# Attention with part of its exponentials made on VectorE, in a statically scheduled rewrite

## The chip, the cores and the metric

One core of one Trainium2 chip. The metric is device time in microseconds (us) from start to end of one execution; lower is better. Engines carry the profile's short names where lines of it are shown: PE (TensorE, matrix multiply), PEld (its weight loads), ACT (ScalarE), DVE (VectorE), POOL (GpSimd), SP (the queue that starts transfers). A ratio below is the mean time of one kernel's fast runs over that of the other's fast runs of the same rounds, so it is not quite the ratio of the medians that are quoted.

## The reference, cut to what matters

Two attention branches over the same input, 2048 positions, 512 features, 32 heads of 16, mixed by a gate.

```python
q, k, v = ...(x @ A_wqkv)                       # branch A: full attention
scores = einsum("bhqd,bhkd->bhqk", q, k) * (16 ** -0.5)
a = einsum("bhqk,bhkd->bhqd", softmax(scores), v) ... @ A_wo
# branch B: the same with 8 keys per query (every second of the last 16 positions)
b = ... @ B_wo
g = sigmoid((x * gate_w).sum(-1))
return g * a + (1 - g) * b
```

Branch A needs 32 x 2048 x 2048 exponentials. The kernels count them in units of 128 keys x 512 queries of one head; there are 2048 units. Branch B is small and runs on GpSimd beside it.

## The kernel before

A unit is a score matmul (32 rows of the array, one of four row positions), an exponential, and a value matmul (17 of 32 columns, one of four column positions) that adds into an accumulator. Three units share one exponential instruction. All of branch A's exponentials run on ScalarE.

```python
def emit_qk(k, dup):                            # one set of three units
    ring = ps.tile([128, maxn, QW], FP32, tag=("rA" if k % 2 == 0 else "rB"), ...)
    for s_, (c_, i, t, j) in enumerate(us):
        mm(ring[:, s_, :], kt_all[32*j:32*j+32, i, t*128:(t+1)*128], qt[32*j:32*j+32, :], True, True, ...)
    pT = work.tile([128, maxn, QW], BF16, tag="pT", ...)
    A.activation(out=pT[:, 0:nu, :], in_=ring[:, 0:nu, :], func=ACT.Exp, scale=float(DH) ** -0.5)

def emit_junk():                                # "filler": nobody reads the result
    jt = misc_ps([128, QW])
    mm_ct(jt, ident[:], ones_t[:], True, True)  # four matmuls, one per column position

# in the loop over sets, where no projection work is at hand:
    if cost < cfg["fill_min"] and k < nsets:
        emit_junk()
```

The order of every engine's instructions is fixed at build time by a loop over the sets. PSUM holds two score buffers of three banks, one scratch bank and the accumulator.

Of the kernel before, what the change touches and what calls it, by code (L numbers as in the profile page):

```python
# [1 line left out]

# [10 lines left out]
BF16 = mybir.dt.bfloat16  # L13
PSUM = bass.MemoryType.PSUM

CFG = dict(
    set_units=3,
    pt_bufs=4,
    burst_budget=2,
    fill_min=1,  # L20
    pv_lag=2,
    enable_b=True,
    chain=("pe", "dve", "act", "pool", "sp"),
    split_dma=False,
)

H = 32
DH = 16
# [4 lines left out]
NEG = -1.0e9  # L33


def _ap(base, dims):
    return bass.AP(tensor=base.tensor, offset=base.offset, ap=[list(d) for d in dims])


@with_exitstack  # L40
def kernel(
# [12 lines left out]
    cfg = CFG  # L54
# [3 lines left out]
    assert D == 512 and S % QW == 0  # L58
# [4 lines left out]
    NBG = S // 32  # L63
    BPC = QW // 32
    ENB = cfg["enable_b"]
    SU = cfg["set_units"]
# [5 lines left out]
    def misc_ps(shape, dtype=FP32, tag="misc"):  # L72
        return ps.tile(shape, dtype, tag=tag, bufs=1, name="misc_ps")
# [4 lines left out]
    def chain_on(key, bi):  # L78
        if bi is None or not hasattr(bi, "ins"):
            return bi  # L80
        if key in cfg["chain"] and prev_inst.get(key) is not None:
            tc.add_manual_dep(bi.ins, prev_inst[key].ins.name, dep_info, reason="program order")
        prev_inst[key] = bi
        return bi

    def chain(bi):
        return chain_on("pe", bi)
# [12 lines left out]

    V = Chained(nc.vector, "dve")
# [4 lines left out]
    def mm(out, lhsT, rhs, start, stop, **kw):  # L106
        return chain(nc.tensor.matmul(out, lhsT=lhsT, rhs=rhs, start=start, stop=stop, **kw))  # L107

    def mm_ct(out, lhsT, rhs, start, stop):
        for c4 in range(4):  # L110
            mm(out[32 * c4:32 * c4 + 32], lhsT[:, 32 * c4:32 * c4 + 32], rhs, start, stop, tile_position=(0, 32 * c4))
# [4 lines left out]

    wst = const.tile([128, DC, 3 * D], BF16, name="wst")
    a_w3 = A_wqkv.rearrange("(c p) n -> p c n", p=128)
    xld_tiles = {}

    def load_x_chunk(sc):
        if sc < 2:
            xl = work.tile([128, W, D], BF16, name="xld", tag="ksh", bufs=2)
        else:
            xl = work.tile([128, NG, QW], BF16, name="xld2", tag="oat", bufs=2)
        eng = SP if (sc % 2 == 0 or not cfg.get("split_dma", True)) else G
        eng.dma_start(out=xl[:, 0:TPC, :], in_=x2d[sc * QW:(sc + 1) * QW, :].rearrange("(t p) d -> p t d", p=128))
        xld_tiles[sc] = xl

    SP.dma_start(out=wst[:, :, D:2 * D], in_=a_w3[:, :, D:2 * D])  # L130
    for sc in range(min(NC, 4)):
        load_x_chunk(sc)
    SP.dma_start(out=wst[:, :, 0:D], in_=a_w3[:, :, 0:D])

    def late_loads():
        SP.dma_start(out=wst[:, :, 2 * D:3 * D], in_=a_w3[:, :, 2 * D:3 * D])
        with nc.allow_non_contiguous_dma(reason="tiny gate vector load"):
            SP.dma_start(out=gw[:], in_=gate_w.rearrange("(c p) -> p c", p=128))
        if ENB:
            SP.dma_start(out=bw[:], in_=B_wqkv.rearrange("(c p) n -> p c n", p=128))  # L140
            SP.dma_start(out=bwo[:], in_=B_wo.rearrange("(c p) n -> p c n", p=128))
        for i in range(NG):
            for j in range(4):
                r0 = (4 * i + j) * DH
                SP.dma_start(out=woarr[32 * j:32 * j + DH, i, :], in_=A_wo[r0:r0 + DH, :])
        if ENB:
            SP.dma_start(out=kv_scr[0:16, 0:D], in_=woarr[16:32, 0, :])
            SP.dma_start(out=kv_scr[0:16, D:2 * D], in_=woarr[16:32, 1, :])

    gw = const.tile([128, DC], BF16, name="gw")  # L150
    if ENB:
        bw = const.tile([128, DC, 3 * D], BF16, name="bw")
        bwo = const.tile([128, DC, D], BF16, name="bwo")
        kv_scr = tc.dram_tile([16 + S, 2 * D], BF16, name="kv_scr")
    woarr = const.tile([128, NG, D], BF16, name="woarr")
    G.memset(woarr[:], 0.0)

    ident = const.tile([128, 128], BF16, name="ident")
    make_identity(nc, ident[:])
    identf = const.tile([NT, NT], FP32, name="identf")  # L160
    make_identity(nc, identf[:])
    ones_t = const.tile([128, QW], BF16, name="ones_t")
    V.memset(ones_t[:], 1.0)
    z32 = const.tile([128, 32], BF16, name="z32")
    V.memset(z32[:], 0.0)
# [5 lines left out]
    for j in range(4):  # L171
        V.memset(selq[32 * j:32 * j + DH, 32 * j + DH:32 * j + DH + 1], 1.0)

    xT = const.tile([128, DC, S], BF16, name="xT")
    kt_all = const.tile([128, NG, S], BF16, name="kt_all")
    vp_all = const.tile([128, NT, H, DH + 1], BF16, name="vp_all")
    G.memset(vp_all[:, :, :, DH:DH + 1], 1.0)
# [3 lines left out]
    g_sp = const.tile([128, NT], FP32, name="g_sp")  # L181
    if ENB:
        omg = const.tile([128, NT], FP32, name="omg")
        maskb = const.tile([128, H, W], FP32, name="maskb")
        G.memset(maskb[:], 0.0)
        G.affine_select(out=maskb[:], in_=maskb[:], compare_op=ALU.is_ge, fill=NEG,
                                base=0, pattern=[[0, H], [-DIL, W]], channel_multiplier=1)

    def k_proj_job(i, sc, ps_tag="misc"):
        st = {}  # L190

        def part(c0, c1, last):
            def s():
                if c0 == 0:
                    st["pk"] = misc_ps([128, QW], tag=ps_tag)
                    mm_init(st["pk"], e32, QW)
                pk = st["pk"]
                for c in range(c0, c1):
                    for j in range(4):
                        h = 4 * i + j  # L200
                        mm(pk[32 * j:32 * j + DH, :], wst[:, c, D + h * DH:D + (h + 1) * DH],
                           xT[:, c, sc * QW:(sc + 1) * QW], False, c == DC - 1, tile_position=(0, 32 * j))
                if last:
                    V.tensor_copy(out=kt_all[:, i, sc * QW:(sc + 1) * QW], in_=pk[:])
                    V.tensor_reduce(out=kmax_all[:, i, sc:sc + 1], in_=kt_all[:, i, sc * QW:(sc + 1) * QW],
                                    axis=AX.X, op=ALU.max, apply_absolute_value=True)
            return s
        return [(3, part(0, 2, False), 0, True), (2, part(2, DC, True), 0, False)]

    def selk_job(i):  # L210
        def s():
            V.tensor_reduce(out=kmax[:, i:i + 1], in_=kmax_all[:, i, :], axis=AX.X, op=ALU.max)
            V.tensor_scalar(out=selk_all[:, i, :], in0=selq[:], scalar1=kmax[:, i:i + 1], scalar2=-1.0,
                                    op0=ALU.mult, op1=ALU.mult)
        return [(0, s, 0, False)]

    def v_proj_job(h0, h1, tb, TB, ps_tag="misc"):
        nh = h1 - h0
        n = nh * DH
        assert TB * n <= 512  # L220
        cost = max(1, (TB * DC * max(n, 96)) // 512)
        st = {}

        def mk(half):
            def s():
                if half == 0:
                    st["pv"] = misc_ps([128, TB, n], tag=ps_tag)
                pv = st["pv"]
                for tt in range(half * TB // 2, (half + 1) * TB // 2):
                    t = tb + tt  # L230
                    for c in range(DC):
                        mm(pv[:, tt, :], xT[:, c, t * 128:(t + 1) * 128],
                           wst[:, c, 2 * D + h0 * DH:2 * D + h1 * DH], c == 0, c == DC - 1)
                if half == 1:
                    V.tensor_copy(out=vp_all[:, tb:tb + TB, h0:h1, 0:DH],
                                  in_=pv[:].rearrange("p t (h d) -> p t h d", d=DH))
            return s
        if TB == 1:
            def s1():
                mk(0)()  # L240
                mk(1)()
            return [(cost, s1, 0, False)]
        return [(max(1, cost // 2), mk(0), 0, True), (max(1, cost - cost // 2), mk(1), 0, False)]

    qt_tiles = {}

    def q_proj_job(c_, i, ps_tag="misc"):
        st = {}

        def s1():  # L250
            p1 = misc_ps([128, QW], tag=ps_tag)
            st["p1"] = p1
            mm_init(p1, z32, QW)
            for c in range(2):
                for j in range(4):
                    h = 4 * i + j
                    mm(p1[32 * j:32 * j + DH, :], wst[:, c, h * DH:(h + 1) * DH],
                       xT[:, c, c_ * QW:(c_ + 1) * QW], False, False, tile_position=(0, 32 * j))

        def s2():  # L260
            p1 = st["p1"]
            for c in range(2, DC):
                for j in range(4):
                    h = 4 * i + j
                    mm(p1[32 * j:32 * j + DH, :], wst[:, c, h * DH:(h + 1) * DH],
                       xT[:, c, c_ * QW:(c_ + 1) * QW], False, c == DC - 1, tile_position=(0, 32 * j))
# [688 lines left out]
```

## Time and profile before

Median 1026.06 us of three runs (1018.97 to 1027.02).

| before | value | where it is read |
|---|---|---|
| ScalarE busy | 937.0 of 1019.7 us | engine table |
| one exponential set of three | 1491 ns long; 1.36 us from start to start | groups; 929 us / 683 |
| ScalarE busy from 200 to 800 us | 96% | stretches |
| filler matmuls | 1156 (289 groups of four) | groups |
| granted clock | 0.973 | cores |

One group of VectorE that has two inputs in SBUF, in a 200 us stretch with GpSimd 88% busy and in one with GpSimd idle (grouped lines of the kernel before for 200 to 400 us, then for 800 to 1000 us):

```profile
L98 DVE SCALAR_TENSOR_TENSOR absq<-qt 128x512 bf16<-128x512 bf16 x7 | 8.1, 1161 | 0.2
```

```profile
L98 DVE SCALAR_TENSOR_TENSOR absq<-qt 128x512 bf16<-128x512 bf16 x6 | 4.2, 692 | 0.2
```

The same operation takes 1161 ns beside a busy GpSimd and 692 ns beside an idle one.

### The profile page before, as it was taken

The page shows a single profiled execution, that of the slowest core. Times are in us where ns is not written, and L with a number is a line of the kernel's source. Part 1 is how long each engine was busy: PE and PEld are TensorE (multiplying, and loading weights), DVE is VectorE, ACT ScalarE, POOL GpSimd, SP SyncE. Part 2 cuts the span into 40 slices and gives each one's busy share as a digit, 9 for nine tenths or more (in the row PEclk, how much of TensorE's full clock was granted, in tenths as well). Part 3 has the DMA queues.
Part 4 walks back from the last instruction along what each step waited for, and adds up shares of the span by engine and source line. Part 5 has one row for each costly group of instructions (what it writes and reads, how often), then busy time and mean ns, then how long its engine had stood idle before and what let it go on. Part 6 is the DMA issues. An engine that isn't in the chain of part 4 may idle for free.

```text
span 1019.7 us, 20777 instructions
## 1 busy us (share of the span) xinstructions
PE 761.0 (75%) x8981; PEld 237.9 (23%) x8981; DVE 331.3 (32%) x535; ACT 937.0 (92%) x703; POOL 597.4 (59%) x540
## 2 busy tenths in 40 slices
PE   5887888877787867777777777776777877777775
PEld 2333232322222211121222221111122211111122
DVE  3453655454244423133233423212222311101113
ACT  1787999999999999999899999999999999999995
POOL 2006699878988979989978878997960000000000
PEclk9999999999999999999899999979999999999998
DMA  7002114003103213102200140310100000000000
GB/s 238 23 2 84 63 43 146 2 22 126 51 7 100 74 52 125 42 2 83 94 2 22 63 135 1 125 42 2 42 1 7 17 1 1 1 1 1 2 1 21
DMA packets 44388, 47.52 MB, mean 47 GB/s; under 512 B 2260, under 2 KB 41732, under 8 KB 44296
## 3 DMA queue, kind: packets, MB, share of 16 engines
q1 hardware_dynamic: 44296, 46.19, 13.9%
q8 instruction: 70, 1.15, 0.5%
q14 instruction: 22, 0.18, 0.1%
HBM read 39.86 MB, written 6.33 MB: 45 GB/s over the span
## 4 chain that ended last, share of the span: by engine, by line
ACT 49%; issue 24%; PE 19%; DVE 8%; ACTq 0%; DMA 0%; POOL 0%; POOLq 0%; DVEq 0%
ACT pT L98 48%; PE misc_ps L107 8%; PE ring L107 5%; PE acc L107 5%; DVE accT L98 2%; DVE kt_all L98 1%; DVE ott L98 1%; DVE qt L98 1%; ACT ex L98 1%; PE pxt L594 0%; DVE oat L98 0%; ACT xT L98 0%; PE misc_ps L462 0%; DVE osb L98 0%; DVE lg L98 0%
## 5 line engine op out<-in xcount | busy, mean ns | idle before, releaser
L98 ACT ACTIVATE pT<-ring 128x1536 bf16<-128x1536 f32 (+1 forms) x683 | 929.0, 1490 | 52.9 <-PE ring L107 50.8
L107 PE MATMUL ring<-qt,kt_all 32*128 32x512 bf16 x2048 | 266.1, 390 | 114.6 <-ACT pT L98 113.6
L107 PE MATMUL acc<-pT,vp_all 128*17 128x512 bf16 x2048 | 288.3, 392 | 79.8 <-ACT pT L98 79.4
L98 POOL TENSOR_TENSOR prod<-prod 128x512 f32<-128x512 f32 x192 | 227.2, 1197 | 5.0
L98 POOL TENSOR_TENSOR prod<-ksh,qb 128x512 f32<-128x512 bf16 x128 | 148.0, 1187 | 94.5 <-DVE qb L98 78.3
L107 PE MATMUL misc_ps<-ones_t,ident 128*32 128x512 bf16 x1156 | 171.6, 399 | 3.9 <-DVE obt L98 3.5
L98 POOL TENSOR_TENSOR prod<-vsh,attn 128x512 f32<-128x512 bf16 x128 | 140.8, 1131 | 53.6 <-issue 38.4
L107 PEld LDWEIGHTS <-kt_all 32*128 32x128 bf16 x2048 | 69.4, 91 | 340.1 <-issue 338.8
L107 PEld LDWEIGHTS <-vp_all 128*17 128x17 bf16 x2048 | 78.6, 89 | 269.8 <-issue 256.2
L98 DVE STREAM_TRANSPOSE accT<-acc 128x512 f32<-128x512 f32 x32 | 22.8, 714 | 209.6 <-PE acc L107 209.6
L107 PE MATMUL misc_ps<-xT,wst 128*16 128x512 bf16 x1024 | 81.6, 385 | 5.3 <-ACT xT L98 3.2
L107 PE MATMUL misc_ps<-bw,xT 128*32 128x512 bf16 x768 | 61.3, 386 | 3.9 <-DVE kvs L98 1.8
L98 DVE CAST qt<-misc_ps 128x512 bf16<-128x512 f32 x32 | 22.1, 690 | 113.1 <-PE misc_ps L107 113.1
L107 PE MATMUL misc_ps<-woarr,oat 128*32 128x512 bf16 x512 | 42.3, 401 | 2.6 <-DVE oat L98 2.6
L98 POOL TENSOR_TENSOR ob<-prod 128x512 f32<-128x512 f32 x32 | 41.7, 1304 | 2.5
L107 PEld LDWEIGHTS <-xT 128*32 128x32 bf16 (+1 forms) x1088 | 34.7, 97 | 29.1 <-issue 21.5
L98 DVE CAST kvs<-misc_ps 128x512 bf16<-128x512 f32 x32 | 22.1, 689 | 52.1 <-PE misc_ps L107 52.1
L107 PEld LDWEIGHTS <-ident 128*32 128x32 bf16 x1156 | 33.8, 95 | 15.1 <-issue 13.7
L107 PEld LDWEIGHTS <-wst 128*16 128x16 bf16 x1024 | 29.5, 89 | 32.0 <-issue 14.7
L98 DVE CAST kt_all<-misc_ps 128x512 bf16<-128x512 f32 x32 | 22.1, 690 | 38.3 <-PE misc_ps L107 38.3
L98 DVE TENSOR_TENSOR ott<-accT,rden 128x512 bf16<-128x512 f32 x32 | 32.3, 1009 | 1.1
L98 DVE TENSOR_TENSOR qt<-qt,misc_ps 128x512 bf16<-128x512 bf16 x32 | 22.0, 687 | 30.3 <-PE misc_ps L107 30.3
(71 smaller groups left out, 420.9 us busy)
## 6 DMA issues: line engine op xcount, KB each, us to landing
ksh<-kv_scr SPq DMA_DIRECT2D x16, 1024.0 KB, 7.3
vsh<-kv_scr SPq DMA_DIRECT2D x16, 1024.0 KB, 6.5
kv_scr<-kvs SPq DMA_DIRECT2D x16, 256.0 KB, 2.0
out_dram<-osb SPq DMA_DIRECT2D x16, 128.0 KB, 1.7
wst<-in_A_wqkv_dram SPq DMA_DIRECT2D x3, 512.0 KB
bw<-in_B_wqkv_dram SPq DMA_DIRECT2D x1, 1536.0 KB
xld<-in_A_x_dram SPq DMA_DIRECT2D x2, 512.0 KB, 5.4
xld_70<-in_A_x_dram SPq DMA_DIRECT2D x1, 512.0 KB, 6.7
```

Of the source, the lines that this page charges most:

```text
L98: return chain_on(key, f(*a, **k))
L107: return chain(nc.tensor.matmul(out, lhsT=lhsT, rhs=rhs, start=start, stop=stop, **kw))
```

## The change

The intent is to take ScalarE's load down. For some key tiles, all four heads of a group (four units, called a quad here) are made on VectorE instead. Scaling the score and adding a constant, then storing it as a 16-bit integer, gives the bit pattern of a bf16 number that approximates the exponential: exponent right, mantissa linear. Four such patterns, shifted by different constants, are multiplied by the same values on PE, which adds them up; the sum is smoother than one pattern. I worked its ripple out from the constants: 0.4% at most about its mean.

The order is no longer made by a loop over sets but by a list scheduler that runs at build time with durations of its own, an event simulation inside the kernel file. The filler is gone, except that the rewrite adds 13 groups of four matmuls at the very start (tile `warm`, 52 matmuls). The diff is 2029 lines; this is its core.

```diff
-CFG = dict(set_units=3, pt_bufs=4, burst_budget=2, fill_min=1, pv_lag=2, ...)
+OFFS = (0, 21, 52, 91)
+EXP_MULT = 128.0 * math.log2(math.e) * DH ** -0.5
+EXP_ADD = 128.0 * (127.0 - _mean_log_ratio())
+SHARED = 1.35                      # planned stretch of an addition beside GpSimd
...
+    def make_quad(p, t):
+        for j in range(4):
+            def fill(...):          # score of one head into a scratch bank
+                mm(st["s"][:], kt_all[32*j:32*j+32, i, t*128:(t+1)*128], qt_tiles[...][32*j:32*j+32, :], ...)
+            def conv(...):          # the first bit pattern
+                V.tensor_scalar(out=q["terms"][0][:, j, :], in0=st["s"][:], scalar1=EXP_MULT, scalar2=EXP_ADD,
+                                op0=ALU.mult, op1=ALU.add)
...
+        for k in range(1, len(OFFS)):
+            def term(k=k):          # the shifted ones
+                V.tensor_scalar(out=q["terms"][k][:], in0=q["terms"][0][:], scalar1=float(OFFS[k]), scalar2=None, op0=ALU.add)
+            tops.append(S_.add(Op("DVE", term, dur=610.0 * SHARED + 80.0, ...)))
...
+        for k, term in enumerate(q["terms"]):
+            for j in range(4):
+                emit_pv_mm(p, t, j, term[:, j, :].bitcast(BF16), ...)
...
-    def emit_junk():
-        jt = misc_ps([128, QW])
-        mm_ct(jt, ident[:], ones_t[:], True, True)
...
+        res = "rA" if ring_i[0] == 0 else "rB"     # score buffers of 3 and 2 banks, two scratch banks
+        n = 3 if ring_i[0] == 0 else 2
...
-        V.tensor_tensor(out=ott[:], in0=accT[:], in1=rd_bc, op=ALU.mult)
+            (V if last else G).tensor_tensor(out=ott[:], in0=st["accT"][:], in1=rd_bc, op=ALU.mult)
...
+        while b_next[0] < NT and b_next[0] * 1.9 <= p + 0.5:    # pace of branch B
+            b_tile(b_next[0], now + 2000.0)
```

## The prediction

> **What bounds it now.** ScalarE. In the page's engine table it is busy 937.0 of 1019.7 us (92%). 683 exponentials of three 128x512 units hold it 929 us, so one set of three costs 1.36 us when back to back (each lasts 1.49 us in the groups, but they overlap). The stretches table shows the loss outside: about 31 us before the first set, then 144 of 160 us busy up to 200 us, 97% from 200 to 1000 us, and 12 us of tail. PE is 75% busy, but 1156 of its 8981 matmuls are filler and transposes. VectorE is 32% busy, GpSimd 59% and idle after 760 us. PE would become the limit only if the change adds passes.

> **What the change does.**
> - It moves whole key tiles ("quads", four units) from ScalarE to VectorE. ScalarE drops about 0.46 us per unit (sets of 3 and 2: 1.36 and about 0.94 us, from the measured slope), so 1.85 us per quad.
> - VectorE per quad: four PSUM conversions of 128x512 (0.69 us each as for the other evictions, about 0.61 when they overlap) = 2.5 us, and three 16-bit additions of a constant over 128x2048.[...]
> - PE per quad: four lone score fills and sixteen value matmuls in place of four, about 1.3 us more by pass length (estimate). The filler goes.
> - VectorE's other work falls from 331 to roughly 260 us: the scaling of the output moves to GpSimd, the second final eviction and one bound pass go.
> - The score buffers shrink from 3+3 to 3+2 banks, for a second scratch bank.

> **How many quads.** Balancing ScalarE, (2048-4N)x0.46+~45 us of ends, with VectorE, 260+4.9N, gives N about 100 and 785-800 us if nothing contends and the order fits.

> **What contends.** [...] absq takes 1161 ns between 200 and 400 us, where GpSimd is 88% busy, and 692 ns after 800 us, where it is idle. So each addition should last about 1.0-1.2 us while GpSimd works, against the 0.9 us the new schedule assumes, adding 0.3-1 us per quad[...]. The instruction order is fixed at build time, so late additions stall PE, and PE then starves ScalarE. PE itself is nearly full. I charge 50-60 us for this.

> **Prediction.** 850 us, 8 in 10 between 790 and 925. Faster by over 2%: 0.93; within 2%: 0.04; slower: 0.03.

> **What would show it.** Groups: about 80-115 quads, i.e. 320-460 conversions of about 0.69 us and 240-345 additions with mean 0.9-1.2 us in GpSimd's stretch and about 0.7 outside it; exponential sets of two and three, about 1600-1700 units. Engine table: ScalarE 87-95% busy, VectorE 80-95%, GpSimd 75-90% with its work spread to nearly the end. Chain of waits: ScalarE falls below its 49%; VectorE and PE grow. First exponential set at 20-30 us.

> **What would make it wrong.** [...] If contention is mild and the schedule fits, 790-810 us. If PE's changes between row and column tiling cost more than planned, ScalarE idles waiting for scores.

The sum came to 785-800 us for the balance, taken as 795, plus a charge of 50-60 us, taken as 55: 850 us. Of the 4.9 us a quad in the balance, 2.5 are the conversions; the other 2.4, by difference, are for the three additions, and no run had shown one. That additions lengthen beside GpSimd as absq does was my assumption. The other unit costs can be read in the trace of the kernel before: VectorE operations of 0.69 us follow each other in 0.60 to 0.61 us where the later one does not wait for the earlier, and PE passes of 512 columns, four matmuls side by side, follow each other in 0.216 us at full clock (by estimate four lone fills and four passes of values in place of two passes, so six more, 1.3 us).

## More of the kernel before

"Granted clock" is the share of full speed that the profile's clock records give for PE.

From the page of the kernel before, the engine table and the time line in 40 equal slices (each digit is the busy share in tenths; PEclk is the granted clock in tenths):

```profile
PE 761.0 (75%) x8981; PEld 237.9 (23%) x8981; DVE 331.3 (32%) x535; ACT 937.0 (92%) x703; POOL 597.4 (59%) x540
...
PE   5887888877787867777777777776777877777775
...
DVE  3453655454244423133233423212222311101113
ACT  1787999999999999999899999999999999999995
POOL 2006699878988979989978878997960000000000
PEclk9999999999999999999899999979999999999998
```

ACT reads 9 nearly everywhere: ScalarE is the limit. DVE is two thirds idle, which is the room that the change wants to use. POOL is dense for three quarters of the time.

The costliest group and the filler, from the page of the kernel before (columns: line, engine, operation, tiles, shapes, count | busy us, mean ns | idle before, and what ended it):

```profile
L98 ACT ACTIVATE pT<-ring 128x1536 bf16<-128x1536 f32 (+1 forms) x683 | 929.0, 1490 | 52.9 <-PE ring L107 50.8
...
L107 PE MATMUL misc_ps<-ones_t,ident 128*32 128x512 bf16 x1156 | 171.6, 399 | 3.9 <-DVE obt L98 3.5
```

## The result, and the profile after

The change runs in 976.36 us (median of 4, 971.36 to 978.63) against 1023.99 us for the kernel before in the same rounds: ratio 0.9529 (95% interval 0.9485 to 0.9574), faster. Executions over 1.5% slower than the fastest of the same kernel are left out of the means. The prediction of 850 us was too low by 126 us, and the result lies outside its range of 790 to 925 us.

From the page of the changed kernel, the same lines as above:

```profile
PE 826.1 (85%) x8922; PEld 250.4 (26%) x8922; DVE 772.8 (79%) x1097; ACT 796.8 (82%) x709; POOL 690.5 (71%) x570
...
PE   7989878998899889888899888889889988987961
...
DVE  3757699898887998789897788889787869799760
ACT  3868748999888889998999878897989978898850
POOL 1340679849589796367984689769686499699686
PEclk9989988999689987887989786796879979798695
```

No row is 9 throughout any more. ScalarE has 140 us less to do, but its idle time did not fall with it: its busy share went from 92 to 82%. PEclk has fallen from 9 to between 5 and 9; the mean is 0.863 against 0.973. The chain of waits of this page can't be used: it stops after 2% of the span.

The groups that answer to those of before, and the two new groups of VectorE (page of the changed kernel):

```profile
L300 ACT ACTIVATE pT<-ring 128x1024 bf16<-128x1024 f32 (+2 forms) x683 | 784.8, 1264 | 127.7 <-PE ring L300 107.0
...
L300 DVE TENSOR_SCALAR dt<-dt 128x2048 uint16<-128x2048 uint16 x261 | 305.9, 1208 | 2.3
L300 DVE TENSOR_SCALAR dt<-m_ps 128x512 uint16<-128x512 f32 x348 | 231.4, 682 | 90.3 <-PE m_ps L300 59.6
```

348 conversions and 261 additions are 87 quads. ScalarE's idle time before exponentials went from 53 to 128 us, and 107 us of it ended when PE delivered scores. An addition took 1208 ns.

What a half-speed stretch looks like (time line of the changed kernel, first PE, then ScalarE; start us, length us of the group, engine, what, [idle before, and what ended it]):

```profile
607.05 0.60 PE L300 MATMUL m_ps<-qt,kt_all 32*128 32x512 bf16 x1
607.06 1.03 PE L300 MATMUL ring<-qt,kt_all 32*128 32x512 bf16 x3
608.01 0.62 PE L300 MATMUL m_ps<-ones_t,zpad 128*32 128x512 bf16 x4
608.41 1.07 PE L300 MATMUL m_ps<-xT,wq 128*16 128x512 bf16 x8
609.42 0.61 PE L300 MATMUL ring<-qt,kt_all 32*128 32x512 bf16 x2
...
613.67 0.40 PE L300 MATMUL acc<-pT,vp_all 128*17 128x512 bf16 x4
614.00 0.39 PE L300 MATMUL m_ps<-qt,kt_all 32*128 32x512 bf16 x2
```

```profile
606.69 1.02 ACT L300 ACTIVATE pT<-ring 128x1024 bf16<-128x1024 f32 x1 [2.06 <-PE ring L300]
608.18 1.45 ACT L300 ACTIVATE pT<-ring 128x1536 bf16<-128x1536 f32 x1 [0.47 <-PE ring L300]
610.12 1.02 ACT L300 ACTIVATE pT<-ring 128x1024 bf16<-128x1024 f32 x1 [0.49 <-PE ring L300]
```

What additions and GpSimd products look like beside each other (time line of the changed kernel, first VectorE, then GpSimd):

```profile
703.19 3.01 DVE L300 TENSOR_SCALAR dt<-dt 128x2048 uint16<-128x2048 uint16 x2
```

```profile
703.06 5.62 POOL L300 TENSOR_TENSOR prod<-vsh,lg 128x512 f32<-128x512 bf16 x4
```

Two additions take 3.01 us and four GpSimd products take 5.62 us, 1.40 each. An addition takes 0.70 us with GpSimd emptied (e2, below), a product 1.07 us in a stretch of the kernel before where VectorE is mostly idle (4.27 us for four).

The end of the changed kernel (time line of ScalarE, GpSimd and PE): the last exponential of branch A ends at 941 us, and then

```profile
930.98 10.06 ACT L300 ACTIVATE pT<-ring 128x1536 bf16<-128x1536 f32 x9 [1.15 <-PE ring L300]
...
957.06 4.26 POOL L300 TENSOR_TENSOR prod<-vsh,lg 128x512 f32<-128x512 bf16 x4
961.28 3.82 POOL L300 TENSOR_TENSOR prod<-prod 128x512 f32<-128x512 f32 x3
965.17 1.26 POOL L300 TENSOR_TENSOR obb<-ob,prod 128x512 bf16<-128x512 f32 x1
...
966.49 0.62 PE L300 MATMUL m_ps<-ident,obb 128*32 128x128 bf16 x16 [19.05 <-POOL obb L300]
```

PE waits 19 us for GpSimd to end the last tile of branch B. The tail after the last exponential is 34 us; in the kernel before it was 10 us. The tail differs much between the runs below, so the end of the last exponential and the tail have to be read apart.

The scheduler gives a yardstick of its own. Its event simulation, which runs when the kernel is built, ends at 879 us for the changed kernel, with 87 quads, VectorE busy 672 us and PE 615 us. It assumes full clock and an addition of 0.90 us. So the chip ran 97 us later than the plan. Below, "plan" means this number; it is arithmetic of the kernel file, not a measurement, and it is trusted here only because runs below land near it (e1 2% over, e5 1% under, e10 2% over).

### The profile page after: what moved, and what is told of

It is laid out like the page before. It is cut to its first block, busy times and chain, and to the rows that moved or that the text cites. A ratio compares the mean times of both kernels' runs of the same rounds, so it can differ in the third digit from the quotient of the medians.

```text
span 975.1 us, 21187 instructions
## 1 busy us (share of the span) xinstructions
PE 826.1 (85%) x8922; PEld 250.4 (26%) x8922; DVE 772.8 (79%) x1097; ACT 796.8 (82%) x709; POOL 690.5 (71%) x570
## 5 line engine op out<-in xcount | busy, mean ns | idle before, releaser
L300 ACT ACTIVATE pT<-ring 128x1024 bf16<-128x1024 f32 (+2 forms) x683 | 784.8, 1264 | 127.7 <-PE ring L300 107.0
L300 PE MATMUL ring<-qt,kt_all 32*128 32x512 bf16 x1700 | 319.7, 424 | 69.5 <-ACT pT L300 65.4
L300 DVE TENSOR_SCALAR dt<-dt 128x2048 uint16<-128x2048 uint16 x261 | 305.9, 1208 | 2.3
L300 DVE TENSOR_SCALAR dt<-m_ps 128x512 uint16<-128x512 f32 x348 | 231.4, 682 | 90.3 <-PE m_ps L300 59.6
L300 POOL TENSOR_TENSOR prod<-prod 128x512 f32<-128x512 f32 (+1 forms) x208 | 268.2, 1301 | 5.8
L300 POOL TENSOR_TENSOR prod<-vsh,lg 128x512 f32<-128x512 bf16 x128 | 161.5, 1291 | 96.5 <-issue 94.9
L300 PE MATMUL acc<-pT,vp_all 128*17 128x512 bf16 x1700 | 182.0, 424 | 0.0
L300 PE MATMUL m_ps<-qt,kt_all 32*128 32x512 bf16 x348 | 132.5, 439 | 15.6 <-DVE dt L300 12.2
L300 PE MATMUL acc<-dt,vp_all 128*17 128x512 bf16 x1392 | 118.6, 466 | 5.1 <-DVE dt L300 5.0
L300 PE MATMUL m_ps<-bw,xT 128*32 128x512 bf16 x768 | 58.2, 404 | 2.2 <-DVE kvs L300 1.8
```

What stands on the lines that cost most here:

```text
L300: return chain_on(key, f(*a, **k))
```

## The experiments

Theories. **Contention** (the expectations call it the port theory; no run shows by what means it comes about): additions and GpSimd's operations make each other longer (1.21 us for an addition on the mean, 1.40 us for a product, as above), VectorE and branch B run late against the fixed order, and the in-order engines wait. **Clock**: without the filler, PE has stretches of little work, its clock is halved there, and then PE is too slow to feed ScalarE. **Order**: the rewritten order is bad in itself. All edits are to the changed kernel unless said otherwise, and each was timed in 3 rounds. Medians of before in the same rounds were 1022 to 1027 us.

| run | edit | us | ratio to before | clock | plan |
|---|---|---|---|---|---|
| the change | | 976.36 | 0.9529 | 0.863 | 879 |
| e1_no_quads | no quads | 1476.98 | 1.4407 | 0.651 | 1446 |
| e2_no_gpsimd | branch B emptied on GpSimd (wrong result) | 914.85 | 0.8914 | 0.879 | 879 |
| e3_zero_filler | filler | 959.38 | 0.9359 | 0.950 | 892 |
| e4_before_no_filler | kernel before, filler off | 1055.77 | 1.0297 | 0.788 | |
| e5_no_gpsimd_filler | e2 and e3 (wrong result) | 883.85 | 0.8641 | 0.994 | 892 |
| e6_scale_on_vector | output scaling back on VectorE | 985.05 | 0.9605 | 0.848 | 865 |
| e7_honest_additions | additions planned at 1.21 us | 1006.98 | 0.9837 | 0.832 | 923 |
| e8_selective_filler | filler only where the plan is thin | 966.78 | 0.9453 | 0.869 | 881 |
| e9_wide_values | value matmuls 32 columns wide | 977.98 | 0.9536 | 0.854 | 879 |
| e10_two_terms_filler | two patterns per quad, filler | 867.91 | 0.8483 | 0.976 | 853 |
| e11_decoupled | nobody waits for branch B (wrong result) | 961.37 | 0.9360 | 0.855 | 879 |
| e12_two_terms | two patterns per quad | 928.06 | 0.9113 | 0.863 | 866 |
| e13_filler_same_order | filler unknown to the scheduler | 973.43 | 0.9514 | 0.949 | 879 |
| e14_no_gpsimd_filler_same_order | e2 and e13 (wrong result) | 906.03 | 0.8831 | 0.967 | 879 |

### The rewrite without quads

```diff
-        if e == "PE" and d_busy[0] < 2:
+        if False and e == "PE" and d_busy[0] < 2:
```

> The rewrite with no unit moved to VectorE (all 2048 exponentials on ScalarE, sets of 3 and 2). If the rewritten order is sound in itself, ScalarE bounds it: 410 pairs of sets x 2.30 us + about 45 us of ends = 985 to 1010 us, ScalarE over 93% busy. If the rewritten order itself (lost filler, 3+2 banks) starves ScalarE, over 1030 us with the granted clock clearly under the 0.973 of before. Clock theory: PE has less to do here than in the change and no filler, so the clock is at or under 0.86. Port theory: [...] VectorE is never late and the clock should be near 0.97.

It took 1477 us at a clock of 0.651. By number that is the second expectation (over 1030 us, a low clock), but by a cause that I had not named. The plan itself is 1446 us: without quads the scheduler makes an order in which ScalarE waits 350 us for the small softmax of branch B, and PE 368 us for GpSimd. So this run says nothing about clock or contention. It says that the order is not robust: the list scheduler turned a lighter problem into a plan 567 us longer, and the chip followed the plan to about 2%.

### Emptying GpSimd

The order of all other engines is unchanged; 33 GpSimd operations per tile of branch B become two memsets.

```diff
+            fn = lg_zero if n_ == 17 else obb_zero if n_ == 32 else (lambda: None)
             o = Op("POOL", fn, dur=dur, ...)
```

> Wrong result on purpose: the changed kernel in its exact order, but GpSimd's 33 operations per tile of branch B are replaced by two memsets, [...] branch B is never late. Port theory: additions fall from 1208 to about 690 ns, VectorE is never late, the clock returns to over 0.95 and the time to 830 to 870 us. Clock theory (the lost filler alone lowers the clock): additions fall likewise, but the clock stays under 0.90 and the time is 900 to 950 us (only the 20 us of GpSimd tail and some VectorE time come back).

914.85 us, 61 us less, with the clock at 0.879. The group of additions (grouped lines of this run):

```profile
L300 DVE TENSOR_SCALAR dt<-dt 128x2048 uint16<-128x2048 uint16 x261 | 173.2, 701 | 2.3
```

701 ns against 1208 ns: the additions are longer because GpSimd works, as the contention theory has it, and GpSimd's work is worth 61 us in all (the waits for branch B included). Its further claim, that the low clock is only a consequence, fell: the clock hardly moved. The clock theory had named this outcome. 36 us are left over the plan.

### The filler put back

Four matmuls with zero weights add nothing to the accumulator ahead of each batch of value matmuls; the scheduler knows of them.

```diff
+        for j in range(4):
+            mm(acc_tiles[periods[p]][32*j:32*j+32, :], z32, ones_t[:], False, False, tile_position=(0, 32*j))
         for (_, t, j, _, grp, s_) in batch:
```

> The changed kernel with a filler put back: four matmuls by zero weights accumulate nothing into the value accumulator ahead of each batch of value matmuls (about 425 groups, 92 us more PE work at full clock, known to the scheduler). Clock theory: granted clock back over 0.95, time 900 to 945 us in spite of the extra work. Port theory: the clock may rise, but PE only gets more work and the time stays at 970 to 1010 us.

The 92 us are an estimate: 425 passes of 0.216 us, the planned length of a pass, which is also what the traces of before and the change show at full clock.

The clock came back to 0.950 and the time fell to 959.38 us, between the ranges of the two theories (900 to 945 and 970 to 1010 us). The filler is PE work too (about 425 groups). The trace says where the gain lies: the last exponential still ends at 939 us (941 in the change; with 85 quads ScalarE has 8 units, about 4 us, more to do), and the tail is 18 us instead of 34. From 200 to 800 us (the change, then this run; columns: us, then busy us and instruction counts of PE, PEld, DVE, ACT, POOL, then clock, DMA share, GB/s):

```profile
200.00:800.00 600.00, 529.24 (x5524) 150.32 (x5527) 505.20 (x698) 531.38 (x471) 442.15 (x357) 0.85 0.15 46
```

```profile
200.00:800.00 600.00, 542.00 (x6637) 155.77 (x6640) 494.11 (x682) 533.42 (x472) 459.18 (x375) 0.95 0.16 48
```

ScalarE ran 471 and 472 instructions in these 600 us. So beside a working GpSimd the higher clock gave ScalarE next to nothing; this run's gain is an earlier end of branch B, under another plan.

### The kernel before without its filler

```diff
     def emit_junk():
+        return
```

> The kernel before without its 289 minus 0 filler groups (matmuls whose result nobody reads). Clock theory: the granted clock falls from 0.97 to under 0.90 and the time rises by 1 to 6%. Rival: filler only fills idle PE time, clock over 0.95, time within 1% of 1024 us or lower.

1055.77 us, 3.0% slower, with the clock at 0.788. Nothing else in the source differs, and the tail is 10 us in both, so this is the cleanest evidence for the clock theory: less PE work made this kernel slower. In the change the filler went too, with no line of my sum for it. The stretch from 200 to 800 us of the kernel before, then of this run (columns: us, then busy us and instruction counts of PE, PEld, DVE, ACT, POOL, then clock, DMA share, GB/s):

```profile
200.00:800.00 600.00, 450.09 (x5310) 130.56 (x5307) 192.04 (x309) 576.65 (x437) 491.03 (x439) 0.97 0.16 52
```

```profile
200.00:800.00 600.00, 472.31 (x4351) 123.03 (x4345) 191.88 (x305) 561.37 (x422) 492.42 (x442) 0.76 0.16 51
```

959 matmuls fewer, and yet PE is busy longer and ScalarE less.

### Both losses removed

> Wrong result on purpose: GpSimd's branch B emptied as in e2 and the zero filler of e3. The scheduler's own plan for this order ends at 892 us. If the plan plus these two losses (port, clock) account for the change's time, it lands on its plan: 890 to 905 us, clock over 0.95, ScalarE waiting under 60 us for scores. If a third loss of the size of the other two is left, 925 us or more.

883.85 us at a clock of 0.994, 8 us under its plan of 892 us and 6 us below the expected range. No third loss shows between plan and chip. It is not excluded, though: the plan counts 0.90 us for an addition and a working branch B, and this run had 0.71 us and none. The filler is worth 31 us here against e2 (884 and 915 us), and here it is ScalarE that gains: the last exponential ends at 867 us against 897. From 200 to 800 us e2 had

```profile
200.00:800.00 600.00, 540.17 (x5822) 155.08 (x5813) 426.26 (x729) 553.43 (x493) 34.71 (x45) 0.88 0.17 52
```

The stretches of this run:

```profile
0.00:40.00 40.00, 33.88 (x453) 14.52 (x453) 17.77 (x36) 21.15 (x21) 4.13 (x12) 1.00 0.55 179
40.00:200.00 160.00, 152.28 (x2089) 55.89 (x2090) 122.23 (x218) 128.74 (x115) 8.31 (x10) 1.00 0.12 38
200.00:800.00 600.00, 563.83 (x7226) 167.73 (x7225) 438.44 (x743) 578.86 (x520) 37.91 (x48) 0.99 0.19 56
800.00:866.00 66.00, 59.09 (x753) 17.80 (x753) 46.47 (x76) 61.23 (x56) 3.99 (x4) 1.00 0.01 2
866.00:880.00 14.00, 5.42 (x104) 2.46 (x92) 6.14 (x11) 0.89 (x2) 0.00 (x0) 0.86 0.11 39
```

This is close to what the prediction should have started from. From 200 to 800 us ScalarE is 96% busy and PE 94%; VectorE only 73%. ScalarE is idle 19 us before 40 us, 31 us from 40 to 200 us where the projections keep PE 95% busy, 26 us from 200 to 866 us and 13 us at the end. The conversions on VectorE (grouped lines of this run):

```profile
L300 DVE TENSOR_SCALAR dt<-m_ps 128x512 uint16<-128x512 f32 x340 | 229.6, 686 | 128.0 <-PE m_ps L300 72.3 <-PE ring L300 54.4
```

VectorE is idle 128 us before them, nearly all of it until PE delivers scores.

### Output scaling back on VectorE

```diff
-            (V if last else G).tensor_tensor(out=ott[:], ...)
+            V.tensor_tensor(out=ott[:], ...)
```

> The scaling of the output (31 operations of 1.15 us) goes back from GpSimd to VectorE; plan 865 us against 879. Coupling theory: GpSimd waits 73 us in its queue for VectorE to get to these, which makes branch B late and leaves a 20 us tail; without them that wait is gone, GpSimd ends before ScalarE and the time is 935 to 955 us. Rival: VectorE is the tight engine, 31 more operations with two SBUF inputs make it later, 975 us or more.

A miss: 985.05 us, no gain, and the rival's range. The tail did shrink (17 us after the last exponential against 34), but the last exponential came at 967 us instead of 941. This order also differs from the change's as a whole (plan 865 us), so it does not settle what a single scaling costs.

### The plan with the true length of an addition

```diff
-SHARED = 1.35
+SHARED = 1.85
```

> Only the planned length of an addition is changed, from 0.90 us to the measured 1.21 us (SHARED 1.85); the plan is then 923 us with 81 quads. If the change loses by running late against its plan, the time moves towards its plan plus the clock loss: 945 to 965 us, below the 976 of the change. If lateness costs little, fewer quads make it slower: 985 to 1010 us.

1006.98 us: slower than the change, in the rival's range (against the kernel before, ratio 0.9837, unclear at 2%). But not for the rival's reason alone: the last exponential ended at 946 us against 941, and 26 of the 31 us are a longer tail (60 us against 34), in which branch B ends. The plan became 923 us with 81 quads, and the chip was still 84 us behind it, with additions at 1160 ns. Telling the scheduler the truth about one duration removed neither the long additions nor the low clock (0.832).

### Filler only where the plan is thin

> The zero filler only where the plan has under 24 matmuls of 512 columns in the last 3.4 us; plan 881 us[...]. Clock theory [...]: clock 0.92 to 0.96 and 945 to 960 us, at least as good as e3. If a sparse filler does not hold the clock (the plan is not where the chip is), clock under 0.90 and 965 us or more.

966.78 us (median of the three fast runs, 961.76 to 975.23) and a clock of 0.869: the miss that the second expectation named. This filler did not hold the clock. Whether that is because the thin stretches of the chip are not those of the plan, or because 58 groups are too few against 427 in e3, was not separated.

### Wider value matmuls

```diff
-        mm(acc[32*j:32*j+DH+1, :], vp_all[:, t, 4*i+j, :], rhs, ...)
+        mm(acc[32*j:32*j+32, :], vp_flat[:, g0:g0+32], rhs, ...)     # 32 columns, the last 15 read by nobody
```

> Same order and same number of matmuls as the change, but each value matmul uses 32 columns of the array instead of 17 (the 15 more land in rows that nobody reads). If the granted clock follows how much of the array works, it rises over 0.90 and the time falls to 945 to 965 us for free. If it follows only how many columns stream through in a window, the clock stays at 0.85 to 0.87 and the time at 970 to 980 us.

977.98 us, clock 0.854 (0.863 in the change). Using more columns of a tile did not raise the clock.

### Two patterns per quad instead of four

One addition in place of three and eight value matmuls in place of sixteen, with and without the filler of e3.

```diff
-OFFS = (0, 21, 52, 91)
+OFFS = (0, 65)
```

> Two shifted bit patterns instead of four (one addition per quad in place of three, eight value matmuls in place of sixteen), with the zero filler; less exact. Plan 853 us with 107 quads. If additions [...] are the main loss, it lands close to its plan: 870 to 895 us, clock over 0.95. If GpSimd's lateness or something else dominates, 920 us or more.

> Two shifted bit patterns as in e10 but without the filler; plan 866 us with 113 quads. This completes the square of terms by filler. If the filler's gain holds here too (17 us with four terms, more where the port loss is smaller: 31 us without GpSimd), the clock is under 0.90 and the time 885 to 910 us. If fewer additions alone keep PE fed and the clock up, over 0.95 and 865 to 880 us.

867.91 us with the filler, 15 us over its plan, the fastest correct kernel of this study; 928.06 us without it. The price is exactness: the ripple of two patterns, worked out as for four, is 1.5% at most against 0.4%. The outputs are right. e12 missed its range (885 to 910 us) on the slow side: the two differ by 60 us. Little of that is in the main work. In the profiled runs (866.55 and 921.53 us) the last exponential ends at 833 us with the filler and at 844 us without; the other 45 us are the tail, 32 us against 76, in which GpSimd finishes branch B. The two plans also differ (853 and 866 us, 107 and 113 quads). The engine table and the slices of e10:

```profile
PE 787.3 (91%) x9926; PEld 244.8 (28%) x9926; DVE 637.7 (74%) x1023; ACT 755.3 (87%) x675; POOL 646.6 (75%) x570
...
ACT  3765989889999889999999999999999899999940
...
PEclk9999899999999999999989999999999999999985
```

### GpSimd works, but nobody waits for it

The small softmax of branch B works on a constant tile and the transposes read zeros; every order is that of the change.

```diff
-            A.activation(out=st["lg"][:], in_=st["lg"][:], func=ACT.Exp)
+            A.activation(out=maskb[:], in_=maskb[:], func=ACT.Exp)
...
-                              in_=st["obb"][:, ...],
+                              in_=zpad[:, ...],
```

> Wrong result on purpose: GpSimd does all its work [...], in the same order, but nobody waits for it: the small softmax of branch B works on a constant tile and the transposes read zeros. Port theory: additions stay at 1.15 to 1.2 us, the 20 us tail goes, 945 to 960 us. Rival (the 61 us of e2 are waits of the in-order engines for a late branch B): additions stay as long but the time falls to 910 to 930 us.

961.37 us, additions at 1165 ns. Waits for a late branch B are worth 15 us (12 of them in the tail, 22 us against 34), which leaves about 46 of the 61 us of e2 for the contention itself. What GpSimd still delivers here, the scaling of the output, can't be a hidden wait: VectorE waited 3 us for it in all. This landed 1 us above the contention theory's range and far from the rival's.

### The filler without a change of order

e3 and e5 carried another plan. To take that out, the filler was put in without telling the scheduler.

> The zero filler of e3, but unknown to the scheduler, so that order and quads (87, plan 879 us) are exactly those of the change. Clock theory: clock over 0.94 and 935 to 955 us, 20 to 40 us under the change. If e3's gain came from its other plan (85 quads) and not from the clock: 970 us or more although the clock rises.

> Wrong result on purpose: e13 with GpSimd's branch B emptied as in e2; order of the change. With e2 (915), e13 and the change (976) it makes a square in one order. If port and clock are all that separates the change from its plan: 870 to 890 us, clock over 0.97. If something else is left: 905 us or more.

973.43 us and 906.03 us: both miss the clock theory's range and fall where the rival put them. The clock rose to 0.949 and 0.967, and the time fell by only 3 us (within the noise) and 9 us. A likely reason, not shown, is that a filler of this density gives back about what it earns: it adds about 425 groups, about 90 us by an estimate (a pass at full speed takes 0.216 us from start to start in the trace of the changed kernel), while the half-speed time that it removes (from 270 to 101 us) is worth at most half of 169 us. GpSimd's work is worth about the same in this pair (973.43 - 906.03 = 67 us) as in the other (61 us); between e3 and e5 it is 76 us. The price of the low clock cannot be read from a filler run of the changed kernel. And e14, with both disturbances removed in the change's own order, is still 27 us over the plan of 879 us; whether the filler that this plan does not know is the whole reason stays open.

## Why the prediction was wrong

**The result as a sum.** 976 us = 879 us plan + 61 us contention and lateness (change minus e2) + 36 us left in e2 over the same plan. The 36 us I put down to the clock: PE at 0.879 is the one slowdown against the plan that I see in e2, and when the clock is restored inside a plan (e5) nothing is left. That is an argument from what remains, not an isolated measurement; e14, which restored the clock without a plan for the filler, won only 9 us of them. Nor do the two losses simply add: with GpSimd emptied the planned filler won 31 us (e2 to e5), but with GpSimd working it moved the last exponential by only 2 us (e3). So the split holds for this order of removal, the contention first. The prediction had 795 us + 55 us.

- **What bounds the kernel before**: right. ScalarE, 1.36 us per set.
- **Costs per operation**: right. Conversions 682 ns (said 0.69 us). Exponentials of three and two units start 1.33 to 1.35 and 0.90 to 0.92 us apart where they overlap in the changed kernel (said 1.36 and 0.94 us). Additions 701 ns with GpSimd emptied (e2; said about 0.7 us), 1208 ns on the mean beside GpSimd (said 1.0 to 1.2 us), from 0.65 to 1.82 us. 87 quads (said 80 to 115). First exponential at 26 us (said 20 to 30). The busy shares all came out below what was said: ScalarE 82% (87 to 95), VectorE 79% (80 to 95), GpSimd 71% (75 to 90).
- **"N about 100 and 785-800 us if nothing contends and the order fits"**: this is the step that failed most. Without contention and at full clock the kernel takes 884 us (e5, with 85 quads and an order planned for 0.90 us an addition), 84 to 99 us more. From e5: ScalarE has 791 us of work, not 758, as 85 quads in place of 100 leave it 60 units (28 us at 0.46 us) more and branch B's exponentials were not counted (8 us); and it is idle 89 us, not 45. I balanced two engines, ScalarE and VectorE, and wrote "PE itself is nearly full" only as a remark. In e5 VectorE sits idle for 128 us before its conversions, nearly all of it until PE delivers scores, so in this order VectorE is not filled to the level that the balance needed. Whether PE's capacity or the order of its instructions sets that was not separated: PE is 94% busy in e5, but with some 90 us of filler (estimate above), and the plan of the change counts PE busy for only 615 of 879 us. I had also charged no idle time to the projection stage, where 31 us are lost.
- **"I charge 50-60 us" for contention**: right in kind and size. Each makes the other longer, 701 against 1208 ns for the addition, 1.07 against 1.40 us for a GpSimd product; by what was not shown. The total was 61 us (67 us in the second pair), the waits for branch B among them. GpSimd's work ended at 966 us and left a tail of 34 us against 16 in e2.
- **"The filler goes"**: wrong in sign (and the 1156 matmuls are all filler; the transposes are other groups). I counted it as relief for PE. It held PE's clock: removing it alone took the clock of the kernel before from 0.973 to 0.788 and cost 3.0% (e4). The prediction had no term for the clock. In the changed kernel it is about 36 us by the sum above, which is argued and not measured alone.
- **"What would make it wrong"**: none of the things listed was shown to be it. An addition took 1208 ns on the mean. ScalarE did wait for scores (107 us), as the last point has it, but no run shows that changes of tiling were the reason; the plan, which counts 0.1 us for such a change, was met in e5.

What stays open: by what additions and GpSimd's operations lengthen each other, the exact price of the low clock in the changed kernel, what keeps ScalarE idle for 89 us even in e5, and why the scheduler's plans jump by tens of microseconds under small edits (865 to 923 us among e3 to e9, 1446 us in e1).

**How the clock behaved.** I divided all profiled executions into windows of 3.413 us, the step of the clock records, and worked out in which share of each window at least one matmul was streaming. The share is an estimate from the start times: 0.21 us for a matmul of 512 columns, other widths in proportion, and twice that at half speed (in the traces of before and the change, matmuls of 512 columns on the same column position follow each other in 0.216 us at full clock and 0.427 us at half, the median); overlaps counted once; windows from the first clock record on. Over all sixteen profiles (before, the change and e1 to e14):

| streaming share of a window | at full clock: next window at half | at half clock: next window at half |
|---|---|---|
| 0.3 to 0.4 | 143 of 145 | 9 of 9 |
| 0.4 to 0.5 | 124 of 281 | 21 of 21 |
| 0.5 to 0.6 | 48 of 480 | 108 of 108 |
| 0.6 to 0.7 | 0 of 541 | 233 of 233 |
| 0.7 to 0.8 | 0 of 879 | 131 of 148 |
| 0.8 to 0.9 | 0 of 923 | 123 of 370 |
| 0.9 to 1.0 | 0 of 53 | 2 of 129 |

In these profiles a window at full clock was followed by half clock in 143 of 145 cases at a share of 0.3 to 0.4, in 124 of 281 at 0.4 to 0.5 and in none of 2396 above 0.6. A window at half clock was followed by full clock in none of the 371 cases of the table below 0.7, in 17 of 148 at 0.7 to 0.8, 247 of 370 at 0.8 to 0.9 and 127 of 129 above. In the middle of the two rows where the outcome turns, at 0.45 of full and 0.85 of half speed, about the same number of columns streams per window: 3700 and 3500, by estimate from 3.413 us and 0.21 us for 512 columns at full clock, twice that at half. So a share that kept the full clock did not restore it: windows with a share of 0.6 to 0.8 were followed by full clock in all of 1420 cases at full clock, but at half clock 364 of 381 were followed by half clock again. By what rule the clock is set was not shown.

## What to carry to other kernels

Before removing matmuls that seem to do nothing, look at the granted clock: work that fills PE's gaps may be what keeps its clock at full, and dropping it can cost more than it saved (0.973 to 0.788 and 3.0% of the time in the kernel before). Putting filler back is no sure gain: it has to be read at the engine that limits the kernel, and in the changed kernel beside a working GpSimd that engine gained nothing. When work moves to an idle engine, balance all engines that the moved work touches, here PE's score fills and the GpSimd products that lengthen beside the additions (1.07 to 1.40 us), and not only the giver and the taker. A static order is worth what its durations are worth; compare its own end time with the chip, remove the suspected disturbances one by one, and see whether the chip lands on the plan. Read the end of the main work and the tail apart: most of the gain of e3, and of the gap between e10 and e12, was tail.
